# Row maxima as bias and 64-column exponentials for the second block of local attention, in a fused attention and squared-ReLU kernel

## The chip, the cores and the metric

One core of one Trainium2 chip runs the kernel. The metric is the device time of one execution in microseconds. The kernel before was timed in 3 runs: 785.89, 786.21 and 788.44 us, median 786.21 us.

## What is computed

```python
# attention within chunks of 64 tokens: B, H, S, D = 8, 8, 576, 64
scores = scale * np.matmul(q_c, k_c.transpose(0, 1, 2, 4, 3))        # scale = 1 / sqrt(64)
scores = scores - np.max(scores, axis=-1, keepdims=True)
attn = np.exp(scores)
attn = attn / (np.sum(attn, axis=-1, keepdims=True) + 1e-09)
out = np.matmul(attn, v_c)
...
# then on x = out as 4608 tokens x 512
h = x @ w_in                                                          # 512 -> 2048
r = np.maximum(h, 0.0)
g = s * (r * r) + b
return (g @ w_out).astype(np.float32)                                 # 2048 -> 512
```

## The kernel before

All matrix products keep fp32 accuracy: the weights and the tokens are each split into a high part `hi` and a low part `lo`, and a product is three matmuls. The 4608 tokens go through in columns of 512. The first 512 are done in a start-up stage (`Layer`: `up0` to `up15`, `down0` to `down15`) while the weights come in from HBM and are converted: `load` (DMA), `scale` and `tail` (ScalarE), `shift` and `sign` (VectorE), `add` (GpSimd), `hi` (ScalarE), `lo` (VectorE). Sixteen loads k = 0 to 15 are converted in this way, the first in halves `0a` and `0b`. The raw words lie in a pool of 3 buffers, so that `load3` waits until `add0a` and `add0b` have read load 0. The converted weights are written back to HBM (`in`, `out` steps, by DMAs on SyncE's queue) and streamed from there for the 4096 remaining tokens, which are done in four blocks of 1024 with seven products in the place of eight.

The softmax of the first 512 tokens can't hide behind earlier matmuls. It is done by two objects of class `Early`: `one` (tokens 0 to 255) and `two` (tokens 256 to 511), each in two halves i = 0 and 1 of 128 tokens with 8 heads. The steps of a half are: `scores` (TensorE, 32 matmuls of 64x64, line 464), `peak` (VectorE, the row maximum, line 470), `sub` (VectorE, scores less maximum, PSUM to SBUF, line 476), `exp` (ScalarE, one instruction of 128x512, line 480), `sum` (VectorE, line 486), `normz` (VectorE, two small instructions, lines 490 and 491), `norm` (VectorE, line 495), `transposes` (TensorE, line 504), `copies` (ScalarE, line 509), `values` (TensorE, line 516), and `x_hi` (ScalarE, line 524) with `x_lo` (VectorE, line 528), which give the split tokens that the up products read. `up0a` and `up1a` are the up products of columns 0 to 255 (they need `one`), `up0b` and `up1b` of columns 256 to 511 (they need `two`).

PSUM has 8 banks of 512 fp32 columns. At the start they are: `ps_p`, two pairs; `ps_a`, one pair; `ps_h`, two single banks. A half's scores take 256 columns in each bank of a pair, so that the two halves of a block share their two banks; the second half's scores wait until the reader of the first half's has done, since an instruction waits for users of the same bank. `one.scores` and `one.values` use the first pair of `ps_p`, `two.scores` and `two.values` the second, the transposes of both use `ps_a`.

The order of the work is written out by hand: `ORDER` (lines 19 to 73) is a list of names, called one by one, and each engine runs its own instructions in that order. `keep_busyN` (line 124) issues N matmuls of 128x128 on constant data that nobody reads; each of the N shows as two records in the trace. `s_and_b` puts the scalars s and b on all partitions by two tiny transposes on TensorE, and `sb` copies them out on VectorE. Loads and stores are issued by SyncE in the order of the list; a store that waits holds what stands behind it.

Of the kernel before, what the change touches and what calls it, by code (L numbers as in the profile page):

```python
# [30 lines left out]
g_hi3 three.norm down0 scale4 g_lo1 hi3 shift4 relu2 g_lo3 three.transposes sign4 square2
g_hi2 down1 load6 lo3 tail5 scale5 add4 g_lo2 in2 three.copies up4 shift5
hi4 sign5 tail6 load7 four.scores lo4 relu4 scale6 add5 up5 out1 four.peak
square4 five.load_qk g_hi4 four.sub hi5 shift6 down2 load8 g_lo4 relu5 sign6 tail7
scale7 lo5 three.values four.exp add6 in3 square5 up6 four.sum three.x_out g_hi5 shift7
hi6 g_lo5 down3 sign7 relu6 square6 four.normz g_hi6 load9 add7 tail8 g_lo6
up7 scale8 four.norm hi7 lo7 four.transposes relu7 square7 load10 shift8 up8 scale9
in4 lo6 four.copies sign8 g_hi7 tail9 down4 shift9 out2 add8 g_lo7 relu8
square8 tail10 up9 g_hi8 sign9 load11 hi8 g_lo8 add9 scale10 down5 relu9
square9 g_hi9 shift10 hi9 lo8 five.scores sign10 out3 down6 scale11 load12 five.peak  # L40
six.load_qk add10 tail11 g_lo9 five.sub down7 hi10 shift11 lo9 five.exp sign11 in5
four.values lo10 tail12 up11 add11 five.sum scale12 load13 five.load_v out4 four.x_out five.normz
hi11 up10 shift12 five.norm x21.hi relu11 sign12 x11.hi down8 x21.lo relu10 square11
add12 square10 load14 g_hi11 g_hi10 five.transposes g_lo11 scale13 g_lo10 down9 five.copies x11.lo
hi12 shift13 lo11 tail13 six.scores sign13 in6 up13 lo12 scale14 add13 six.peak
load15 out5 tail14 seven.load_qk six.sub up12 relu13 square13 shift14 ring0 six.exp s_add1
hi13 down10 sign14 relu12 g_hi13 lo13 square12 tail15 add14 g_lo13 five.values in7
g_hi12 six.sum scale15 down11 g_lo12 five.x_out six.normz shift15 hi14 six.load_v six.norm up14
sign15 ring1 lo14 up15 add15 out6 relu14 square14 g_hi14 g_lo14 hi15 down12
s_add0 ring2 s_hi1 lo15 s_hi0 s_add7 relu15 six.transposes out7 square15 down13 g_hi15  # L50
s_add5 six.copies s_lo0 six.values s_lo1 s_keep0 g_lo15 down14 six.x_out s_add6 s_keep1 x22.hi
xt1.add_dve seven.scores x22.lo xt1.hi seven.load_v down15 xt3.add_dve eight.load_qk xt1.lo xt3.hi xt2.add_dve p1.0
st2 st1 xt3.lo xt2.hi p2.0 seven.peak u1.0 st0 p1.1 xt2.lo st3 c11.0
p5.0 u1.1 xt4.add_dve relux.0 p6.1 s_add3 xt4.hi p6.0 u2.1 seven.sub p7.1 xt4.lo
ring3 u2.0 seven.exp s_add2 p7.0 u3.1 p2.1 seven.sum u3.0 c22.0 p4.0 seven.normz
c11.1 p3.0 s_add4 c21.0 relux.1 sqx.0 p4.1 ring4 c12.0 seven.norm s_hi2 p1.2
c21.1 s_lo2 split0.hi p5.1 seven.turn0 s_keep2 u1.2 sqx.1 p6.2 reluy.0 c22.1 p2.2
split0.lo u2.2 ring5 sqy.0 seven.turn1 p3.1 split1.hi p7.2 c11.2 s_hi3 seven.turn2 relux.2
p1.3 ring6 u3.2 c12.1 p4.2 seven.turn3 reluy.1 p5.2 u1.3 sqy.1 s_lo3 seven.values
eight.scores ring7 c21.2 c22.2 sqx.2 s_keep3 split1.lo p3.2 seven.x_out eight.peak eight.load_v nine.load_qk  # L60
p2.3 eight.sub s_hi4 c12.2 p6.3 eight.exp c11.3 reluy.2 eight.sum p5.3 ring8 relux.3
s_lo4 sqy.2 p1.4 eight.normz u2.3 s_keep4 eight.norm p2.4 u1.4 eight.turn0 p6.4 p7.3
c11.4 u2.4 eight.turn1 relux.4 p7.4 u3.3 c22.3 p4.3 u3.4 eight.turn2 p3.3 ring9
c21.3 sqx.3 eight.turn3 p1.5 s_hi5 c12.3 p4.4 ring10 s_lo5 u1.5 reluy.3 p5.4
s_keep5 c21.4 sqy.3 eight.values nine.scores c22.4 sqx.4 p3.4 eight.x_out nine.load_v nine.peak p6.5
nine.sub s_hi6 ring11 c12.4 p2.5 nine.exp s_lo6 reluy.4 p1.6 c11.5 ten.load_qk s_keep6 u2.5
nine.sum relux.5 p7.5 sqy.4 nine.normz u1.6 p5.5 nine.norm u3.5 nine.turn0 p4.5 ring12
# [1138 lines left out]
```

## Time and profile before

| | |
|---|---|
| median of 3 runs | 786.21 us |
| the profiled execution's own time | 787.31 us |
| its span (first to last instruction) | 785.3 us |
| TensorE busy | 772.5 us, 98% |
| VectorE busy | 615.6 us, 78% |
| ScalarE busy | 470.2 us, 60% |
| GpSimd busy | 48.6 us, 6% |
| matmuls of the up product j = 1, columns 256 to 511, start | 31.52 us |

An engine's busy time is an average over very different stages. The instructions that the change adds and removes run in the first 35 us; so the tables by stretch and the engines' instructions in order of time are read for the start. Times in rows are in us from the start of the span unless marked ns; the duration of an instruction reaches past the start of the next one on the same engine where the two overlap, so that the distance between starts ("pitch") is what an engine pays in a row of instructions.

### The profile page before, as it was taken

Reading aid. Unit: us, or ns where it says so; the run is one execution under the profiler, and the core shown is the slowest. Engines: PE = TensorE matmul, PEld = TensorE weight load, DVE = VectorE, ACT = ScalarE, POOL = GpSimd, SP = SyncE. Lnnn points to the kernel's source line nnn. Section 1 sums busy time; section 2 is a strip of 40 time slices with the busy share of each in tenths; the row PEclk is TensorE's granted clock in tenths of the full one; section 3 lists DMA queues with packets and bytes.
Section 4 is the critical chain, followed back from the end, with each engine's and each line's share of the span. In section 5 each row is a group of like instructions: output and inputs, shape, how many; then the busy total and the mean of one; then the engine's idle time right before and its main releaser. Section 6 shows DMA issues by size and latency. Waiting matters only on the chain.

```text
span 785.3 us, 13873 instructions
## 1 busy us (share of the span) xinstructions
PE 772.5 (98%) x5584; PEld 639.2 (81%) x5584; DVE 615.6 (78%) x891; ACT 470.2 (60%) x645; POOL 48.6 (6%) x23
## 2 busy tenths in 40 slices
PE   6899999999999999999999999999999999999998
PEld 6787887888888888888888888888888888888886
DVE  5998999998569986888899858888998723348773
ACT  3899877777653433566864635666846346565442
POOL 1443440000000000000000000000000000000000
PEclk9999999999999999999999999999999999999999
DMA  9999998778568999876566587666565778886653
GB/s 360 343 349 337 362 314 307 234 241 270 183 218 293 307 352 332 320 269 222 181 214 208 194 299 290 247 260 205 175 224 179 243 262 293 297 269 214 206 195 135
DMA packets 79844, 204.33 MB, mean 260 GB/s; under 512 B 5796, under 2 KB 39076, under 8 KB 68516
## 3 DMA queue, kind: packets, MB, share of 16 engines
q1 hardware_dynamic: 79488, 203.18, 74.4%
q8 instruction: 44, 0.72, 0.4%
q10 hardware_dynamic: 292, 0.26, 0.1%
q14 instruction: 20, 0.16, 0.1%
HBM read 159.38 MB, written 44.04 MB: 259 GB/s over the span
## 4 chain that ended last, share of the span: by engine, by line
PE 83%; DMA 6%; DVE 5%; ACT 3%; issue 1%; POOL 0%; POOLq 0%; SPq 0%; DVEq 0%; ACTq 0%
PE ps_h L690 22%; PE ps_h L910 17%; PE ps_o L690 17%; PE ps_x L910 8%; PE ps_x L609 6%; PE ps_o L910 4%; PE ps_h L609 3%; PE ps_o L609 3%; DMA raw<-in_w_dram 2%; PE ps_a L368 1%; PE ps_x L424 1%; DMA w_in<-t 1%; DVE t L198 1%; DMA w_out<-t 1%; DVE t L182 1%; ACT t L172 1%
## 5 line engine op out<-in xcount | busy, mean ns | idle before, releaser
L690 PE MATMUL ps_h<-t,raw 128*128 128x512 f32 x672 | 167.4, 391 | 0.0
L690 PEld LDWEIGHTS ps_h<-t,raw 128*128 128x128 f32 x672 | 125.4, 188 | 26.5 <-ACT u L700 0.2
L910 PE MATMUL ps_h<-t,raw 128*128 128x512 f32 (+1 forms) x588 | 142.4, 385 | 0.0
L884 DVE TENSOR_TENSOR t<-t 128x512 fp32r<-128x512 f32 (+1 forms) x120 | 105.5, 900 | 33.2 <-ACT t L882 33.1
L910 PEld LDWEIGHTS ps_h<-t,raw 128*128 128x128 f32 x588 | 108.8, 188 | 22.2
L709 DVE TENSOR_TENSOR t<-ps_o,u 128x512 f32<-128x512 f32 x96 | 66.0, 690 | 75.7 <-PE ps_o L690 70.3
L690 PE MATMUL ps_o<-t,raw 128*128 128x512 f32 x480 | 121.8, 389 | 0.0
L690 PEld LDWEIGHTS ps_o<-t,raw 128*128 128x128 f32 x480 | 90.1, 188 | 18.8
L700 ACT COPY u<-ps_h 128x512 f32<-128x512 f32 x96 | 56.0, 585 | 69.5 <-PE ps_h L690 68.6
L882 ACT CAST t<-t 128x512 fp32r<-128x512 f32 (+1 forms) x120 | 87.4, 789 | 2.8 <-PE ps_h L910 1.9
L412 DVE STREAM_TRANSPOSE pT<-p 32x256 f32<-32x256 f32 x192 | 83.7, 436 | 3.2
L910 PE MATMUL ps_x<-t,raw 128*128 128x512 f32 x288 | 73.2, 390 | 0.0
L753 ACT ACTIVATE t<-t 128x1024 f32<-128x1024 f32 x64 | 67.2, 1053 | 0.2
L910 PEld LDWEIGHTS ps_x<-t,raw 128*128 128x128 f32 x288 | 54.0, 188 | 11.5 <-DMA raw<-w_out 0.3
L749 ACT ACTIVATE t<-t 128x512 f32<-128x512 f32 (+1 forms) x64 | 54.1, 846 | 10.3 <-DVE t L709 9.8
L190 POOL TENSOR_TENSOR t<-t,raw 128x1024 int32<-128x1024 int32 (+1 forms) x17 | 47.9, 2820 | 69.0 <-DVE t L184 39.1
L609 PE MATMUL ps_x<-t,raw 128*128 128x512 f32 x192 | 48.9, 390 | 0.0
L634 PE MATMUL ps_h<-x,t 128*128 128x512 f32 (+1 forms) x216 | 47.5, 371 | 1.3 <-DVE x L528 0.7
L914 ACT ACTIVATE u<-ps_h,shift,sb 128x512 f32<-128x512 f32 x18 | 13.1, 779 | 58.2 <-PE ps_h L910 58.2
L634 PEld LDWEIGHTS ps_h<-x,t 128*128 128x128 f32 x216 | 37.0, 188 | 8.9 <-DVE x L528 1.0
L609 PEld LDWEIGHTS ps_x<-t,raw 128*128 128x128 f32 x192 | 36.0, 188 | 7.5
L910 PE MATMUL ps_o<-t,raw 128*128 128x512 f32 x144 | 36.5, 389 | 0.0
(129 smaller groups left out, 1014.7 us busy)
## 6 DMA issues: line engine op xcount, KB each, us to landing
raw<-w_in SPq DMA_DIRECT2D x42, 1024.0 KB, 6.0
raw<-w_out SPq DMA_DIRECT2D x34, 1024.0 KB, 5.3
raw<-w_sum SPq DMA_DIRECT2D x24, 1024.0 KB, 5.0
raw<-in_w_dram SPq DMA_DIRECT2D x15, 1024.0 KB, 7.9
qk<-in_qkv_dram SPq DMA_DIRECT2D x15, 1024.0 KB, 8.2
w_out<-t SPq DMA_DIRECT2D x16, 512.0 KB, 6.6
w_sum<-t SPq DMA_DIRECT2D x16, 512.0 KB, 9.1
v<-in_qkv_dram SPq DMA_DIRECT2D x15, 512.0 KB, 4.6
```

What stands on the lines that cost most here:

```text
L190: nc.gpsimd.tensor_tensor(out=i, in0=i, in1=low.bitcast(I32), op=ALU.add)
L412: nc.vector.transpose(out=self.pT[k].rearrange("p i a t -> p (i a) t")[:, :, t], in_=p[t, :, k])
L609: nc.tensor.matmul(out=self.ps[m], lhsT=x, rhs=y, start=(j == 0 and i == 0), stop=(j == stop and i == 2))
L634: nc.tensor.matmul(out=self.ps[j][:, cols], lhsT=w[:, c, :], rhs=x[:, c, :], start=(c == 0 and i == 0), stop=(c == NHP - 1 and i == 2))
L690: nc.tensor.matmul(out=ps, lhsT=w[:, e, :], rhs=y[:, e, :], start=start and e + i == 0, stop=e + i == 3, skip_group_check=not start)
L700: nc.scalar.copy(out=u, in_=self.a[p])
L709: nc.vector.tensor_tensor(out=self.tile(p, h)[:, e, :], in0=ps, in1=u, op=ALU.add)
L749: nc.scalar.activation(out=t, in_=t, func=AF.Relu)
L753: nc.scalar.activation(out=t, in_=t, func=AF.Square)
L882: nc.scalar.copy(out=hi, in_=f)
L884: nc.vector.tensor_tensor(out=lo, in0=f, in1=hi.bitcast(F32), op=ALU.subtract)
L910: nc.tensor.matmul(out=self.acc[name][m][:, cols], lhsT=x, rhs=y[:, cols], start=new and q == 0, stop=q == 2, skip_group_check=not new)
```

## The change

For `two`, the subtraction, the one wide exponential and the sum are replaced. VectorE forms `less`, the row maxima times -1/8 (`bias`, 128x8). ScalarE then makes eight exponentials of 128x64 for each half (`exps`), which read the scores from PSUM, take a column of `less` as bias and write the row's sum through `accum_out`. In `one`, the second half's scores go to a bank pair of their own (`ps_a`, which `one.transposes` uses afterwards), so that they need not wait for `one.sub0`. `two`'s halves still share a pair. `ORDER` is new throughout its length. Its start, both versions, follows; behind it the steps are the same, in a somewhat other order.

```diff
-one.load_qk0 one.load_qk1 three.load_qk load0b load0a two.load_qk0 two.load_qk1 two.load_v one.scores0 one.peak0 one.load_v s_and_b
-sb one.sub0 one.exp0 one.scores1 keep_busy7 load1 one.sum0 one.peak1 three.load_v one.normz0 one.sub1 one.norm0
-one.exp1 four.load_v tail0b one.transposes0 keep_busy3 one.sum1 one.normz1 one.copies0 load2 one.norm1 tail0a scale0a
-one.transposes1 four.load_qk shift0a scale0b two.scores0 keep_busy8 one.copies1 sign0a shift0b add0a two.peak0 two.sub0
-hi0a sign0b two.scores1 two.exp0 lo0a add0b two.peak1 one.values0 keep_busy7 two.sum0 one.x_hi0 two.sub1
-load3 hi0b one.x_lo0 two.exp1 lo0b one.values1 keep_busy4 tail1 two.normz0 in0 two.sum1 scale1
-two.norm0 two.normz1 two.transposes0 keep_busy2 one.x_hi1 shift1 two.copies0 two.norm1 two.values0 sign1 two.transposes1 two.x_hi0
-one.x_lo1 two.copies1 add1 two.x_lo0 up1a scale2 tail2 two.values1 shift2 up0a hi1 sign2
-two.x_hi1 three.scores lo1 add2 two.x_lo1 in1 three.peak scale3 up1b tail3 three.sub up0b
...
+one.load_qk0 one.load_qk1 two.load_qk0 two.load_qk1 four.load_v four.load_qk load0a load0b one.load_v one.scores0 one.peak0 load1
+one.scores1 keep_busy3 s_and_b sb one.sub0 one.peak1 one.exp0 two.load_v two.scores0 keep_busy13 one.sum0 one.sub1
+load2 one.normz0 one.exp1 two.peak0 one.sum1 two.bias0 one.normz1 two.exps0 one.norm0 three.load_v one.transposes0 keep_busy1
+one.norm1 one.transposes1 three.load_qk one.copies0 two.normz0 two.scores1 keep_busy2 one.copies1 two.norm0 scale0a two.peak1 two.transposes0
+keep_busy7 tail0a shift0a two.bias1 sign0a two.exps1 add0a one.values0 keep_busy7 scale0b two.normz1 hi0a
+shift0b one.x_hi0 two.norm1 tail0b lo0a two.transposes1 keep_busy4 scale1 sign0b one.x_lo0 tail1 add0b
+one.values1 keep_busy6 shift1 hi0b load3 one.x_hi1 lo0b two.copies0 sign1 in0 scale2 two.values0
+one.x_lo1 two.copies1 add1 two.x_hi0 up0a tail2 two.x_lo0 two.values1 shift2 hi1 up1a sign2
+two.x_hi1 three.scores lo1 add2 two.x_lo1 in1 scale3 three.peak up1b tail3 three.sub up0b
...
         def scores(self, i):
-            if i == 0:
-                self.ps = self.banks(0)
+            if i == 0 or self.tb == 0:
+                self.ps[i] = self.banks(i)
+            else:
+                self.ps[i] = self.ps[0]
...
+        def bias(self, i):
...
+            nc.vector.tensor_scalar(out=self.less[:, i], in0=self.m[:, i], scalar1=-1.0 / float(D) ** 0.5, scalar2=None,
+                                    op0=ALU.mult)
+
+        def exps(self, i):
...
+            for g in range(NHP):
+                for c in range(2):
+                    n = 2 * g + c
+                    nc.scalar.activation(out=self.p[:, i, g, c, :], in_=self.ps[i][:, c, i, g, :], func=AF.Exp,
+                                         scale=1.0 / float(D) ** 0.5, bias=self.less[:, i, c, g:g + 1],
+                                         accum_out=self.z[:, i, n:n + 1])
```

## Rows read from the trace of the kernel before

**Rows 1.** The page's first lines: span, and busy us (share of the span) with the count of instructions of each engine.

```profile
span 785.3 us, 13873 instructions
PE 772.5 (98%) x5584; PEld 639.2 (81%) x5584; DVE 615.6 (78%) x891; ACT 470.2 (60%) x645; POOL 48.6 (6%) x23
```

**Rows 2.** Busy time by stretch: stretch, its length, busy us of each engine with the number of instructions, granted TensorE clock (1.00 is the higher of its levels), busy share of the DMA engines, GB/s.

```profile
15.00:20.00 5.00, 4.47 (x93) 4.07 (x91) 4.96 (x10) 2.57 (x5) 3.01 (x2) 1.00 1.02 413
20.00:25.00 5.00, 3.67 (x82) 3.14 (x82) 4.93 (x12) 3.85 (x7) 0.00 (x0) 1.00 1.03 422
35.00:40.00 5.00, 5.00 (x23) 3.96 (x22) 4.93 (x7) 5.00 (x9) 3.31 (x1) 1.00 0.96 365
140.00:160.00 20.00, 20.00 (x90) 16.21 (x88) 19.60 (x36) 14.92 (x21) 0.00 (x0) 1.00 0.62 199
```

**Rows 3.** TensorE's matmuls in order of time: start, duration of the whole piece, line, tile, count, and in brackets the idle time before it with what ended it.

```profile
4.53 1.13 PE L464 MATMUL ps_p<-t 64*64 64x64 f32 x32 [4.53 <-DMA t<-in_qkv_dram]
5.59 0.36 PE L1105 MATMUL ps_h<-ident,sb_row 1*128 1x1 f32 x2
7.20 1.13 PE L464 MATMUL ps_p<-t 64*64 64x64 f32 x32 [1.25 <-DVE t L476]
8.26 3.35 PE L126 MATMUL ps_h<-t 128*128 128x128 f32 x14
11.41 1.06 PE L504 MATMUL ps_a<-ident,t 128*128 128x128 f32 x4
...
14.54 2.05 PE L126 MATMUL ps_h<-t 128*128 128x128 f32 x16
17.13 0.69 PE L464 MATMUL ps_p<-t 64*64 64x64 f32 x32 [0.53 <-DVE t L476]
...
31.52 8.47 PE L634 MATMUL ps_h<-x,t 128*128 128x256 f32 x47 [0.29 <-DVE x L528]
...
67.69 2.55 PE L634 MATMUL ps_h<-x,t 128*128 128x512 f32 x10 [0.53 <-DVE t L198]
...
123.96 1.16 PE L424 MATMUL ps_a<-pT,v 64*64 64x64 f32 x64 [0.42 <-ACT pT L417]
```

**Rows 4.** VectorE's instructions in order of time, columns as in rows 3: from the first maximum to the first norm; the first conversion after a pause; the last two ahead of the up product at 31.52.

```profile
5.73 0.69 DVE L470 TENSOR_REDUCE m<-ps_p 128x8 f32<-128x512 f32 x1 [4.73 <-PE ps_p L464]
6.34 0.15 DVE L1168 COPY sb<-ps_h 128x2 f32<-128x2 f32 x1
6.46 0.69 DVE L476 TENSOR_TENSOR t<-ps_p,m 128x512 f32<-128x512 f32 x1
...
9.04 0.16 DVE L490 TENSOR_SCALAR z<-z 128x8 f32<-128x8 f32 x1
...
9.36 0.64 DVE L476 TENSOR_TENSOR t<-ps_p,m 128x512 f32<-128x512 f32 x1
9.92 0.68 DVE L495 TENSOR_TENSOR t<-t,z 128x512 f32<-128x512 f32 x1
...
14.25 0.43 DVE L182 TENSOR_SCALAR t<-t 128x512 uint32<-128x512 uint32 x1 [1.70 <-ACT t L172]
...
29.64 1.22 DVE L198 TENSOR_TENSOR t<-t 128x1024 fp32r<-128x1024 f32 x1
30.78 0.69 DVE L528 TENSOR_TENSOR x<-ps_p,x 128x512 fp32r<-128x512 f32 x1
```

**Rows 5.** ScalarE's instructions in order of time: `one.exp1` with the conversion behind it, one wide `tail`, and `two.x_hi1`.

```profile
10.03 0.63 ACT L480 ACTIVATE t<-t 128x512 f32<-128x512 f32 x1 [2.22 <-DVE t L476]
10.57 0.66 ACT L176 ACTIVATE raw<-raw 128x512 int32<-128x512 uint32 x1
...
27.08 1.16 ACT L176 ACTIVATE raw<-raw 128x1024 int32<-128x1024 uint32 x1
...
29.07 0.58 ACT L524 CAST x<-ps_p 128x512 fp32r<-128x512 f32 x1
```

**Rows 6.** ScalarE's groups by line and shape over the whole span: count, busy us, mean ns of one, idle before. The first two read PSUM with fixed numbers for scale and bias, the last two take both from columns in SBUF.

```profile
L700 ACT COPY u<-ps_h 128x512 f32<-128x512 f32 x96 | 56.0, 585 | 69.5 <-PE ps_h L690 68.6
...
L440 ACT COPY t<-ps_a 128x256 f32<-128x256 f32 x8 | 2.4, 393 | 1.3 <-PE ps_a L424 1.3
...
L914 ACT ACTIVATE o<-ps_h,shift,sb 128x512 f32<-128x512 f32 x4 | 3.1, 779 | 15.3 <-PE ps_h L910 14.7 <-DMA raw<-w_in 0.6
...
L942 ACT ACTIVATE o<-ps_h,shift,sb 128x256 f32<-128x256 f32 x2 | 1.1, 567 | 8.5 <-PE ps_h L910 8.5
```

**Rows 7.** GpSimd's instructions in order of time: `add0a`, `add1`, `add2`.

```profile
15.55 1.34 POOL L190 TENSOR_TENSOR t<-t,raw 128x512 int32<-128x512 int32 x1 [14.25 <-DVE t L184]
...
25.47 2.43 POOL L190 TENSOR_TENSOR t<-t,raw 128x1024 int32<-128x1024 int32 x1 [6.06 <-DVE t L184]
29.86 3.30 POOL L190 TENSOR_TENSOR t<-t,raw 128x1024 int32<-128x1024 int32 x1 [1.95 <-DMA raw<-in_w_dram]
```

**Rows 8.** SyncE's DMA issues in order of time (start, time to issue, line, tile): the q and k of `one`, and `load3`. The lines of times to landing are those of the two loads of `one` (least, median, greatest) and of `load3`.

```profile
0.74 0.85 SPq L452 DMA_DIRECT2D t<-in_qkv_dram  x2
...
19.44 0.33 SPq L157 DMA_DIRECT2D raw<-in_w_dram  x1
...
DMA to landing us min/median/max: 3.7/4.2/4.6
...
DMA to landing us min/median/max: 10.4/10.4/10.4
```

More of the change, by code (lines that the diff above doesn't have):

```diff
@@ L25 @@
-load3 hi0b one.x_lo0 two.exp1 lo0b one.values1 keep_busy4 tail1 two.normz0 in0 two.sum1 scale1
-two.norm0 two.normz1 two.transposes0 keep_busy2 one.x_hi1 shift1 two.copies0 two.norm1 two.values0 sign1 two.transposes1 two.x_hi0
-one.x_lo1 two.copies1 add1 two.x_lo0 up1a scale2 tail2 two.values1 shift2 up0a hi1 sign2
-two.x_hi1 three.scores lo1 add2 two.x_lo1 in1 three.peak scale3 up1b tail3 three.sub up0b
-open_o load4 relu1 shift3 hi2 up3 sign3 relu0 three.exp lo2 square0 square1
-add3 three.sum out0 up2 g_hi0 relu3 g_hi1 load5 square3 three.normz tail4 g_lo0
@@ L31 @@
[L31 to L67, printed above, removed]
@@ new lines @@
+one.x_lo1 two.copies1 add1 two.x_hi0 up0a tail2 two.x_lo0 two.values1 shift2 hi1 up1a sign2
+two.x_hi1 three.scores lo1 add2 two.x_lo1 in1 scale3 three.peak up1b tail3 three.sub up0b
+open_o load4 relu1 hi2 shift3 up3 sign3 relu0 three.exp lo2 square0 square1
+add3 three.sum out0 g_hi0 up2 relu3 g_hi1 load5 square3 tail4 g_lo0 three.normz
+down0 hi3 g_lo1 three.norm scale4 g_hi3 lo3 relu2 three.transposes square2 shift4 in2
+g_hi2 down1 g_lo3 three.copies sign4 tail5 load6 g_lo2 add4 scale5 up5 shift5
@@ new lines @@
+hi4 sign5 four.scores relu5 square5 lo4 load7 scale6 up4 five.load_qk add5 four.peak
+out1 g_hi5 tail6 g_lo5 four.sub down2 relu4 hi5 shift6 sign6 load8 square4
+scale7 lo5 three.values four.exp add6 in3 g_hi4 up7 four.sum three.x_out g_lo4 tail7
+shift7 hi6 up6 four.normz sign7 relu7 square7 four.norm g_hi7 down3 add7 g_lo7
+relu6 load9 scale8 tail8 lo6 square6 four.transposes hi7 shift8 out2 down4 g_hi6
+lo7 four.copies load10 g_lo6 in4 scale9 sign8 five.scores tail9 shift9 add8 up9
+five.peak five.sub six.load_qk hi8 sign9 up8 five.exp load11 lo8 tail10 add9 five.sum
@@ new lines @@
+out3 scale10 down5 relu8 relu9 square8 five.normz square9 shift10 four.values hi9 five.norm
+g_hi9 down6 sign10 g_hi8 five.load_v four.x_out lo9 load12 scale11 add10 g_lo8 in5
+x11.hi five.transposes g_lo9 x21.hi up10 five.copies shift11 x11.lo tail11 sign11 down7 hi10
+relu10 x21.lo square10 load13 scale12 add11 up11 tail12 g_hi10 shift12 hi11 lo10
+six.scores relu11 square11 sign12 out4 tail13 down8 load14 lo11 seven.load_qk g_hi11 scale13
+add12 g_lo10 in6 six.peak up12 g_lo11 six.sub hi12 shift13 down9 six.exp lo12
@@ new lines @@
+relu12 square12 sign13 scale14 up13 six.sum load15 add13 g_hi12 out5 tail14 g_lo12
+down10 shift14 hi13 ring0 s_add1 relu13 square13 lo13 g_hi13 five.values sign14 in7
+tail15 down11 six.normz add14 g_lo13 scale15 five.x_out six.load_v up15 shift15 hi14 six.norm
+ring1 sign15 up14 s_hi1 lo14 relu15 add15 square15 out6 g_hi15 down12 relu14
+g_lo15 square14 g_hi14 s_add6 ring2 hi15 six.transposes g_lo14 lo15 down13 six.copies s_add4
+out7 s_lo1 six.values s_add5 s_keep1 down14 six.x_out s_add0 x22.hi seven.load_v xt1.add_dve seven.scores
@@ new lines @@
+s_hi0 x22.lo xt1.hi down15 eight.load_qk xt3.add_dve s_lo0 xt3.hi xt2.add_dve s_keep0 p1.0 st2
+st1 xt3.lo st3 p2.0 xt2.hi xt1.lo st0 p1.1 u1.0 xt2.lo p5.0 u1.1
+c11.0 s_add2 relux.0 p6.0 xt4.add_dve p2.1 ring3 u2.0 s_add3 xt4.hi p7.0 xt4.lo
+p6.1 u3.0 c11.1 c22.0 p4.0 relux.1 s_add7 u2.1 p3.0 c21.0 seven.peak sqx.0
+p1.2 ring4 c12.0 s_hi2 seven.sub p7.1 reluy.0 s_lo2 u1.2 p5.1 sqy.0 s_keep2
+seven.exp p6.2 split0.hi seven.sum p2.2 u2.2 ring5 split0.lo u3.1 p7.2 c11.2 c22.1
+relux.2 p4.1 seven.normz u3.2 seven.norm p3.1 c21.1 seven.turn0 sqx.1 p4.2 ring6 s_hi3
@@ new lines @@
+c12.1 p1.3 split1.hi s_lo3 c21.2 p5.2 split1.lo reluy.1 s_keep3 sqx.2 seven.turn1 p1.4
+sqy.1 p2.3 ring7 c22.2 u1.3 seven.turn2 p6.3 c11.3 p3.2 u2.3 seven.turn3 relux.3
+p7.3 s_hi4 ring8 c12.2 seven.values eight.scores s_lo4 u3.3 u1.4 reluy.2 s_keep4 sqy.2
+p5.3 eight.peak seven.x_out p6.4 eight.load_v eight.sub nine.load_qk c22.3 p4.3 eight.exp u2.4 eight.sum
+p3.3 ring9 c21.3 sqx.3 eight.normz p7.4 eight.norm s_hi5 c12.3 p1.5 u3.4 eight.turn0
+reluy.3 p2.4 u1.5 sqy.3 s_lo5 p4.4 ring10 c11.4 s_keep5 eight.turn1 p6.5 relux.4
@@ new lines @@
+c21.4 sqx.4 p5.4 eight.turn2 u2.5 p1.6 c22.4 p2.5 eight.turn3 p3.4 c11.5 relux.5
+p7.5 ring11 c12.4 s_hi6 u1.6 p5.5 s_lo6 u3.5 reluy.4 eight.values nine.scores s_keep6
+c22.5 sqy.4 p6.6 ring12 eight.x_out nine.peak nine.load_v p2.6 nine.sub ten.load_qk u2.6 p3.5
+nine.exp c11.6 relux.6 nine.sum p7.6 s_hi7 c12.5 p4.5 nine.normz u3.6 s_lo7 reluy.5
+p4.6 ring13 c21.5 nine.norm sqy.5 s_keep7 p1.7 nine.turn0 sqx.5 p5.6 c21.6 u1.7
+nine.turn1 sqx.6 p6.7 ring14 c22.6 p2.7 u2.7 nine.turn2 p7.7 c11.7 p3.6 nine.turn3
@@ L73 @@
+relux.7 u3.7 d0 ring15 c12.6 reluy.6 p5.7 sqy.6 p4.7 c22.7 p3.7 c21.7
+sqx.7 c12.7 ring16 reluy.7 sqy.7
 """
@@ L463, in scores @@
                     qk = self.qk[i]
-                    nc.tensor.matmul(out=self.ps[cols, c, i, hp, :], lhsT=qk[rows, 0, h, :], rhs=qk[rows, 1, h, :],
+                    nc.tensor.matmul(out=self.ps[i][cols, c, i, hp, :], lhsT=qk[rows, 0, h, :], rhs=qk[rows, 1, h, :],
                                      start=True, stop=True)
@@ L469, in peak @@
                 self.m = att.tile([P, 2, G], F32, name="m%d" % self.tb).rearrange("p i (c g) -> p i c g", c=2)
-            nc.vector.tensor_reduce(out=self.m[:, i], in_=self.ps[:, :, i], op=ALU.max, axis=AX.X)
+            nc.vector.tensor_reduce(out=self.m[:, i], in_=self.ps[i][:, :, i], op=ALU.max, axis=AX.X)
         def sub(self, i):
@@ L475, in sub @@
                 self.p = t.rearrange("p i (g c k) -> p i g c k", g=NHP, c=2)
-            nc.vector.tensor_tensor(out=self.p[:, i].rearrange("p g c k -> p c g k"), in0=self.ps[:, :, i],
+            nc.vector.tensor_tensor(out=self.p[:, i].rearrange("p g c k -> p c g k"), in0=self.ps[i][:, :, i],
                                     in1=self.m[:, i].unsqueeze(3).to_broadcast([P, 2, NHP, CH]), op=ALU.subtract)
@@ L498, in norm_pool @@
             self.norm(i, nc.gpsimd)
+        def bias(self, i):
+            if i == 0:
+                t = self.t = slot()
+                self.p = t.rearrange("p i (g c k) -> p i g c k", g=NHP, c=2)
+                self.less = att.tile([P, 2 * G], F32, name="less%d" % self.tb).rearrange("p (i c g) -> p i c g", i=N, c=2)
+            nc.vector.tensor_scalar(out=self.less[:, i], in0=self.m[:, i], scalar1=-1.0 / float(D) ** 0.5, scalar2=None,
+                                    op0=ALU.mult)
+        def exps(self, i):
+            if i == 0:
+                self.z = att.tile([P, 2 * G], F32, name="z%d" % self.tb).rearrange("p (i g) -> p i g", i=N)
+            self.p3 = self.t.rearrange("p i (g k) -> p i g k", k=CH)
+            for g in range(NHP):
[4 more added lines that the diff above has]
+                                         accum_out=self.z[:, i, n:n + 1])
         def transposes(self, i):
@@ L1135, in local_attention_then_squared_relu_mlp @@
         if isinstance(a, Early):
-            for f in steps + ["load_qk", "x_hi", "x_lo"]:
+            for f in steps + ["load_qk", "x_hi", "x_lo", "bias", "exps"]:
                 for i in range(2):
```

7 lines of the change are left out of this document (1 added, 6 removed).

## The prediction

> **What bounds the kernel now.** First the page's busy shares: TensorE 98% of 785.3 us [rows 1]. Then the table by stretch, to see where it isn't: 20.00 of 20 us from 140 to 160, but 4.47 and 3.67 of 5 in 15 to 25 [rows 2]. Part of that is `keep_busy`, which computes nothing. Third, TensorE's order of time: behind the up product at 31.52 the idle pieces that I read are 0.53 us at 67.69 and 0.42 at 123.96 [rows 3]. So the time is that of the start, up to the up product of `two`'s columns (`up1b`, 31.52), plus a fixed stream. What moves 31.52 moves the end one for one, unless the two later waits give some of it back.
>
> What sets 31.52? It waited 0.29 us for `two.x_lo1` on VectorE, which ran behind `lo1` (29.64 and 30.78) [rows 3, 4]. VectorE was busy 4.96 and 4.93 of 5 us in 15 to 25 while ScalarE had 2.57 and 3.85 [rows 2]. VectorE is the bound of the start, ScalarE has slack. The change moves softmax work from the one to the other.
>
> **Removed from VectorE.** Two `sub` and two `sum` at a pitch of 0.60 (0.69 for one less 0.09 of overlap [rows 4]) are 2.4 us; two `bias` of 128x8 come in at 0.15 (the 128x8 row has 0.16 [rows 4]). Net 2.1 us less in a stretch without holes: the whole of the possible gain.
>
> **Added to ScalarE.** Two `exp` go (0.54 of pitch, 10.03 to 10.57 [rows 5]); sixteen exponentials of 128x64 come. No such row exists. From PSUM with fixed numbers, 512 columns take 585 ns and 256 take 393 [rows 6]: 0.75 per column and 201 fixed, so 249 at 64. With scale and bias from columns, 779 and 567 [rows 6]: 408 at 64. One column costs half the difference, so 329; less 0.09 of overlap, a pitch of 0.24. The sum through `accum_out` is in no row. Free would be 0.24; an instruction of its own, at most another shortest one (0.25), makes 0.49. A result of one column should lie nearer to the fixed part less overlap (0.11) than to 0.25: I take 0.14, so 0.38, 3.05 us for eight. Bounds 1.9 and 3.9. A gain below 0.24 is excluded, as the fixed part is paid by every row.
> The Trainium skill, ScalarE: Activation LUTs, What ACT_TABLE_LOAD costs, gives 280 ns plus 0.833 per column with a bias column and 93 ns of overlap, so an estimate of 1.9 us for eight, and no price for the sum. By it the sum below would end 2 us earlier; it is the low end reached from rows anyway, and still over three times one wide `exp`.
>
> **The bank pair, and what stands in its way.** Before, `one.scores1` waited 1.25 us for `one.sub0` [rows 3]. Now it follows `one.scores0` at once: 0.74 plus half of 0.85 for its issue, 4.6 to land [rows 8], so 5.8, and done at 6.9 (pitch 1.06, 4.53 to 5.59 [rows 3]). But the new list puts `keep_busy3` before `s_and_b`, and `sb` before `one.sub0` on VectorE. Six records at 0.225 (14 in 8.26 to 11.41 [rows 3]) end at 8.2, `s_and_b` (0.36 [rows 3]) at 8.6. VectorE, through with `peak0` at 6.4, stands until then, and `sub0` and ScalarE's `exp0` behind it: `sub0` at 8.7, not 6.46 [rows 4]. This is 2.2 us later, with the wait of 1.25 gone.
>
> **Walk to the new up product.** VectorE from 8.7: `peak1` 9.3, `sum0` 10.1 (after `exp0`: 0.69 + 0.63 [rows 4, 5]), `sub1` 10.7, `normz0` 11.3 (0.32, 9.04 to 9.36 [rows 4]), `two.peak0` 11.6, `sum1` 12.2, `bias0` done 13.0; `normz1`, `norm0`, `norm1` to 14.6. In the kernel before, VectorE stood 1.70 us ahead of 14.25 [rows 4], so the late start is absorbed up to here and two steps of `two` are done as well. From 13.0 the work is ScalarE's, in its order, with 0.5 for a narrow copy (0.58 less 0.09), 0.57 for a narrow and 1.05 for a wide conversion (0.66 and 1.16 less overlap) [rows 5]: `exps0` to 16.05, two copies 17.05, `scale0a` and `tail0a` 18.2 (`bias1` is ready then), `exps1` 21.2, `scale0b` and `hi0a` 22.3, `x_hi0` and `tail0b` 23.3, `scale1` and `tail1` 25.4. `hi0b` needs `add0b`: `lo0a`, `sign0b` on VectorE to 24.1, GpSimd 1.4 (1.34 [rows 7]), so 25.6 to 26.2. `x_hi1` and `two.copies0` 27.2, `scale2` 28.2, `copies1` and `two.x_hi0` 29.2, `tail2` 30.3. `hi1` needs `add1`: `lo0b` at 26.3, `sign1` to 28.1, GpSimd 2.43 or 3.30 [rows 7], mean 2.87, so 31.0; `hi1` 32.0, `lo1` on VectorE 32.1 to 33.25, `two.x_lo1` 33.95. Up product at 34.0 for 31.52: **+2.45 us**. With 0.24 in the place of 0.38 the same walk ends at 32.0 (+0.45; 31.5 and 0.0 with the short add), with 0.49 at 35.8 (+4.3; +4.7 with the long add). Even without any wait ScalarE's own work from 13.0 to `two.x_hi1` is 18.7 us at 0.38 and 16.5 at 0.24.
>
> **What costs nothing, and its cover.** Loads: `load0a` is now the eighth 512 KB, `two.load_v` the thirteenth, `load2` ends with the fifteenth, `three.load_qk` with the eighteenth. At 413 GB/s [rows 2] each takes 1.27 us after the first at 4.5: 13.4, 19.7, 22.3, 26.1. They are wanted at 17.0 (`scale0a`), 28 (`values0`), 27.2 (`scale2`) and after 31. `load3` waits for `add0b`, 25.6 in the place of 19.44, with `in0`, `in1` and `load4` behind it on SyncE's queue. It took 10.4 us then [rows 8], in a queue of 20 units that lasts to 28.6; from 25.6 it lands about 31, before `scale3` (33). If it took 10.4 again, the next conversion would lose 3 us. `keep_busy` grows from 31 to 43 calls, all in holes (TensorE waits 1 us before `two.scores1` for `exps0`, with the transposes of `two` queued behind, and 1.4 before `two.transposes1`); the last six end 2 us before `two.x_lo0` is there. `one.transposes0` waits for `sub1`'s release of `ps_a`, at 11.4, and runs at 14.0: free.
>
> **What follows.** Conversion and TensorE start late together, TensorE is full [rows 2], conversion has some slack, so of the two waits (0.95) I count 0.7 as given back: +2.45 - 0.7 = +1.75. The profiled execution took 787.31 with a span of 785.3, 1.1 above the median; its 789.1 is **788.0** against the median of 786.21. 0.3% (2.36 us) is about what a measurement can tell: 783.85 and 788.57 are the edges.
>
> **Rivals.**
> Cheap sums (0.24): +0.45, less all of the 0.95, gives -0.5: 785.7. For it: ScalarE's idle in 15 to 25 [rows 2]; against it: a sum must leave the engine somehow. Chance 0.20.
> Faster: ScalarE never waits for GpSimd or VectorE, and the sums are free. Its own 16.5 us from 13.0 and `x_lo1` (0.7) bring the up product to 30.3, -1.2, and with 0.95 from the later waits -2.2: 784.0, half of it beyond the edge. It decides from a pitch under 0.28. Chance 0.13.
> Slower, sums dear (0.49): +4.3 - 0.7 = +3.6: 789.8. It crosses the edge from a pitch of 0.42. Chance 0.17.
> Slower by the clock: the clock column reads 1.00 in every stretch [rows 2], yet the 128x128 records went at 0.225 before 11.4 and at 0.12 from 14.54 (16 in 2.05 less the last one's tail) [rows 3], as the lower level (1.2 GHz) against 2.4. If the waits before `two.scores1` and `two.transposes1` bring it down again, `keep_busy4`, `values1`, `keep_busy6` and `two.values0` end at 30.4, 1.7 after ScalarE wants `two.x_hi0`; about +1.3 remain at `hi1`: 789.3. Idle 0.53 at 17.13 left the next 32 matmuls at 0.69 us [rows 3], which speaks against. The Trainium skill, TensorE: Matmul & The Clock Gate, What's actually happening, has the clock fall after idleness; no row here shows a fall. Chance 0.05.
> Mine: 0.45.
>
> **How the numbers follow.** Faster: 0.09 of the faster rival and 0.03 of cheap sums, 0.12. Slower: 0.17 and 0.05, and 0.14 of mine (the upper part, pitch over 0.42 or nothing given back), 0.36. The rest, 0.52, is within 0.3%. The range 784.4 to 790.6 leaves out the far half of the faster rival and the far end of the dear sums.
>
> **What would show it.** `sub0` starting near 8.7 behind `sb`; a pitch of `exps` of 0.38 (0.24, 0.49), or a second instruction behind each; ScalarE without holes from 13 to 31; `up1b`'s columns near 34.0; the waits near 67 and 124 smaller. I am wrong if `sb` isn't late, if the up product starts before 32, or if new waits of TensorE stand behind 35 us, where I followed the new list only in outline.

## The result, and the profile after

The changed kernel takes 793.35 us (median of 7 runs, 790.58 to 797.35), the kernel before 786.99 in the same comparison: a ratio of 1.0085, 95% interval 1.0067 to 1.0104, so 6.4 us slower. The forecast of 788.0 had the sign as its second case and missed the size; the time lies above the range. The profiled execution took 791.22 us with a span of 789.2, 3.9 longer than that of before. It is one of the faster executions of the changed kernel, while the profiled one of before (787.31) lies above its median; so the traces show 3.9 us of the 6.4, and where the rest of it goes isn't shown.

TensorE's order of time in the kernel after, with the rows that answer to [rows 3]:

```profile
5.95 1.14 PE L466 MATMUL ps_a<-t 64*64 64x64 f32 x32
7.02 1.65 PE L126 MATMUL ps_h<-t 128*128 128x128 f32 x6
8.59 0.37 PE L1128 MATMUL ps_h<-ident,sb_row 1*128 1x1 f32 x2
...
9.96 4.50 PE L126 MATMUL ps_h<-t 128*128 128x128 f32 x26
...
33.56 8.49 PE L657 MATMUL ps_h<-x,t 128*128 128x256 f32 x47 [0.30 <-DVE x L551]
...
98.68 2.97 PE L657 MATMUL ps_h<-x,t 128*128 128x512 f32 x12 [0.40 <-DVE t L678]
...
133.64 1.52 PE L713 MATMUL ps_h<-t,raw 128*128 128x512 f32 x6
136.41 1.67 PE L713 MATMUL ps_o<-t,raw 128*128 128x512 f32 x6 [1.26 <-ACT o L636]
...
213.05 1.61 PE L632 MATMUL ps_x<-t,raw 128*128 128x512 f32 x6 [0.30 <-DMA raw<-w_out]
```

The up product of the second 256 columns starts at 33.56 for 31.52 [rows 3], +2.04. The two late waits of before (67.69 and 123.96) are gone, one of 0.40 at 98.68 has come, and the next stage (the first product of the streamed weights, line 713; line 690 before) starts at 133.64 for 131.99, +1.65. Then there are waits that the kernel before hadn't: 1.26 us near 136, and 0.30 for streamed weights near 213. From 220 to 700, TensorE is busy without a hole in both kernels.

VectorE in the start, against [rows 4]; the last two rows shown are `sign2` and `lo1`:

```profile
5.88 0.69 DVE L472 TENSOR_REDUCE m<-ps_p 128x8 f32<-128x512 f32 x1 [4.88 <-PE ps_p L466]
9.00 0.16 DVE L1191 COPY sb<-ps_h 128x2 f32<-128x2 f32 x1 [2.43 <-PE ps_h L1128]
9.08 0.68 DVE L478 TENSOR_TENSOR t<-ps_p,m 128x512 f32<-128x512 f32 x1
...
15.89 0.17 DVE L492 TENSOR_SCALAR z<-z 128x8 f32<-128x8 f32 x1 [1.09 <-ACT t L519]
...
20.65 0.17 DVE L492 TENSOR_SCALAR z<-z 128x8 f32<-128x8 f32 x1 [1.96 <-ACT t L519]
...
30.55 1.23 DVE L184 SCALAR_TENSOR_TENSOR t<-raw,t 128x1024 uint32<-128x1024 uint32 x1
31.69 1.22 DVE L198 TENSOR_TENSOR t<-t 128x1024 fp32r<-128x1024 f32 x1
```

`sub0` starts at 9.08, not 6.46: VectorE stood 2.43 us in front of `sb`. Later it stands 1.09 and 1.96 us for ScalarE's exponentials, where it had been back to back. From 28.59 on it is back to back again.

ScalarE, first two and last of the first eight exponentials, the copies that follow, and `hi1`:

```profile
13.38 0.31 ACT L519 ACTIVATE t<-ps_p,less 128x64 f32<-128x64 f32 x1 [0.98 <-DVE less L508]
13.59 0.19 ACT L519 ACTIVATION_READ_ACCUMULATOR t<-ps_p,less 128x1 f32 x1
13.68 0.30 ACT L519 ACTIVATE t<-ps_p,less 128x64 f32<-128x64 f32 x1
...
15.42 0.35 ACT L519 ACTIVATE t<-ps_p,less 128x64 f32<-128x64 f32 x1
15.62 0.24 ACT L519 ACTIVATION_READ_ACCUMULATOR t<-ps_p,less 128x1 f32 x1
15.71 1.11 ACT L532 COPY pT<-ps_a 128x512 f32<-128x512 f32 x2
...
30.00 1.06 ACT L194 CAST t<-t 128x1024 fp32r<-128x1024 f32 x1 [0.39 <-POOL t L190]
```

Eight take 2.33 us (13.38 to 15.71), a pitch of 0.29. The row's sum is an instruction of its own, 0.19 to 0.24 us long, but it starts 0.1 us before the exponential's record ends.

### The profile page after: what moved, and what is told of

It reads as the page before. It is cut to its first block, busy times and chain, and to the rows that moved or that the text cites. A ratio compares the mean times of both kernels' runs of the same rounds, so it can differ in the third digit from the quotient of the medians.

```text
span 789.2 us, 13945 instructions
## 1 busy us (share of the span) xinstructions
PE 776.5 (98%) x5608; PEld 641.9 (81%) x5608; DVE 612.0 (78%) x889; ACT 474.1 (60%) x675; POOL 47.7 (6%) x23
## 4 chain that ended last, share of the span: by engine, by line
PE 85%; DVE 6%; ACT 4%; DMA 4%; issue 1%; SPq 0%; DVEq 0%; ACTq 0%
PE ps_h L713 22%; PE ps_h L933 17%; PE ps_o L713 16%; PE ps_x L933 8%; PE ps_x L632 6%; PE ps_o L933 4%; PE ps_o L632 3%; PE ps_h L632 3%; PE ps_h L657 2%; DMA w_out<-t 2%; PE ps_a L368 1%; PE ps_x L424 1%; DVE t L198 1%; DMA raw<-in_w_dram 1%; DVE t L184 1%
```

## The experiments

Theory A: the start costs everything, and later waits only follow from it. Theory B: the start costs about 2 us, the new order behind it the rest. Within B, B1 says that each new wait costs its own length, B2 that sums, splits and streamed weights are late by the amount of work and only show in turn; theory C came later and names one misplaced step. "Rest" is the list from `open_o` on. "Up product" is the start of `up1b`, as in the prediction.

| kernel | median us | ratio to before, 95% | up product | next stage | span of the profile |
|---|---|---|---|---|---|
| before (profile shown) | 786.2 | | 31.52 | 131.99 | 785.3 |
| after | 793.35 | 1.0085 (1.0067 to 1.0104) | 33.56 | 133.64 | 789.2 |
| `new_again` | 792.43 | 1.0072 (1.0060 to 1.0083) | 33.84 | 133.20 | 790.4 |
| `new_start_old_rest` | 789.03 | 1.0030 (1.0021 to 1.0040) | 33.35 | 132.98 | 786.6 |
| `old_start_new_rest` | 793.45 | 1.0088 (1.0075 to 1.0101) | 31.42 | 132.88 | 789.6 |
| `softmax_alone` | 792.29 | 1.0074 (1.0055 to 1.0093) | 36.16 | 136.30 | 790.1 |
| `banks_alone` | 786.04 | 0.9995 (0.9984 to 1.0005) | 30.58 | 131.37 | 784.6 |
| `sb_first_old_rest` | 787.59 | 1.0018 (1.0005 to 1.0031) | 32.39 | 132.65 | 785.9 |
| `st_first` | 793.86 | 1.0085 (1.0067 to 1.0103) | 33.75 | 132.99 | 789.1 |
| `d0_later` | 791.83 | 1.0067 (1.0052 to 1.0081) | 33.53 | 134.22 | 789.3 |
| `s_hi1_later` | 790.26 | 1.0050 (1.0034 to 1.0065) | 33.15 | 132.53 | 786.9 |
| `s_hi1_early_in_old` | 789.91 | 1.0042 (1.0028 to 1.0056) | 31.32 | 133.09 | 786.6 |
| `repaired` | 787.17 | 1.0010 (0.9994 to 1.0025) | 31.30 | 129.95 | 783.8 |
| `exps_128` | 786.75 (one execution) | | 30.64 | 131.51 | 784.6 |
| `old_start_repaired_rest` | 787.51 | 1.0001 (0.9989 to 1.0013) | 30.81 | 129.93 | 783.5 |
| `fewer_busy` | 787.40 | 1.0006 (0.9993 to 1.0020) | 31.38 | 130.55 | 784.6 |

The median of before was 786.35 to 786.99 in the comparisons, so ratios compare better than medians. The markers are of one execution each. The first scores start between 4.37 and 4.78 us in these traces, when q and k have landed, and `new_again` reaches the up product 0.28 us after the same kernel did before; so differences of some 0.4 us in the markers aren't told apart.

**The changed kernel again** (`new_again`), nothing edited.

> The changed kernel once more, nothing edited. Its seven times lay between 790.6 and 797.4 us and the profiled one at 791.2, 3.9 above the profile of before: 2.04 of it at the up product of the second 256 columns, the rest in waits behind 90 us. If the wide spread belongs to the kernel, it comes back (791 to 797, with a granted clock under 1.0 in the long ones); if it was of that chip, the times lie within 2 us of 791.

790.7 to 793.6 us, and 1.59 us of waiting near 214 in the place of 0.30. The slowdown is the kernel's; its size moves by some 3 us from execution to execution. The two longest of the first seven (796.9 and 797.4 us, granted clock 0.997 and 0.998) didn't come back.

**The two halves of the list, crossed** (`new_start_old_rest`, `old_start_new_rest`). The edits in short, the first against the kernel after, the second against the kernel before:

```diff
 # new_start_old_rest: new softmax, bank pair, new list up to up0b
-open_o ... (new rest)
+open_o ... (old rest)
 # old_start_new_rest: old softmax and list up to up0b
-open_o ... (old rest)
+open_o ... (new rest)
```

> The new softmax, bank pair and the new list up to up0b, then the old list from open_o on. Theory A (the start costs it all, and the later waits only follow from a late start): 792 to 794. Theory B (the start costs its 2.0 us, the new order behind 35 us costs the rest): 788.5 to 789.5, with the up product of the second columns near 33.6 and the waits behind 60 us as in the kernel before.

> The old softmax and the old list up to up0b, then the new list. Theory A: as before, 786 to 787.5. Theory B: 789.5 to 792, with the up product at 31.5 and the wait for the store of the first columns near 134 us still there.

The new start alone costs 2.4 us (0.30%), the new rest alone 6.8 (0.88%), with the up product at 31.42, as before. Theory A falls; the new rest costs even more than B's 789.5 to 792. The two don't add up: together they cost what the rest costs alone. In `old_start_new_rest` the next stage starts at 132.88, and TensorE waits behind it as in the kernel after:

```profile
135.65 1.66 PE L690 MATMUL ps_o<-t,raw 128*128 128x512 f32 x6 [1.25 <-ACT o L613]
...
213.44 1.62 PE L609 MATMUL ps_x<-t,raw 128*128 128x512 f32 x6 [1.41 <-DMA raw<-w_out]
```

So with the new rest the next stage starts near 133 with either start. That a late start only takes slack from a rest that is late already fits this, but isn't shown by itself.

**The softmax by itself** (`softmax_alone`).

```diff
-two.sub0 ... two.scores1 two.exp0 ... two.sum0 ... two.sub1 ... two.exp1 ... two.sum1
+two.bias0 ... two.exps0 two.scores1 ... two.bias1 ... two.exps1
```

> The old list, in which only the second block's sub becomes bias, its exp the eight narrow exponentials (the first set ahead of its second scores), and its sum goes; no bank pair. ScalarE pays 2 x (2.33 - 0.54) = 3.6 us more, VectorE 2.1 less. If ScalarE's slack between 15 and 25 us covers it, the up product comes 0.5 to 1.5 us earlier and the time is 785.5 to 786.5; if ScalarE has become the bound of the start whatever the order, the up product comes 1 to 2 us later and the time is 788 to 789.

Worse than either answer: up product at 36.16, +4.6. `two.scores1` shares its banks with the first half's scores, and so waits for all eight exponentials, which stand behind the conversions on ScalarE. TensorE's rows (start, duration, idle), and its clock by stretch (stretch, length, busy us with records, granted clock, DMA share, GB/s):

```profile
14.33 2.05 PE L126 MATMUL ps_h<-t 128*128 128x128 f32 x16
19.94 1.13 PE L466 MATMUL ps_p<-t 64*64 64x64 f32 x32 [3.56 <-ACT t L519]
...
21.85 3.35 PE L126 MATMUL ps_h<-t 128*128 128x128 f32 x14
```

```profile
16.00:20.00 4.00, 0.44 (x8) 0.94 1.00 403
20.00:24.00 4.00, 4.00 (x74) 0.50 1.04 430
24.00:28.00 4.00, 4.00 (x53) 0.71 0.99 399
```

After 3.56 us without work the granted clock is 0.50, its lower level, and the same 32 matmuls take 1.13 us in the place of 0.69 [rows 3]. Here the clock rival is seen; the trace agrees with the Trainium skill, TensorE: Matmul & The Clock Gate, What's actually happening, that idleness brings the clock down. In the changed kernel itself the clock column stays at 1.00 behind its short waits, and 14 constant matmuls still take 1.73 us at 17.64 and 1.83 at 19.92, some 0.12 each.

**The bank pair by itself** (`banks_alone`).

```diff
-            if i == 0:
-                self.ps = self.banks(0)
+            if i == 0 or self.tb == 0:
+                self.ps[i] = self.banks(i)
+            else:
+                self.ps[i] = self.ps[0]
```

> The old list and the old softmax, only that the second half of the first block's scores has the bank pair ps_a, so that it needn't wait for the first sub. The wait of 1.25 us at 7.2 goes. If this wait set the start, the up product of the second columns comes up to 1.2 us earlier (30.3) and the time is 785.4; if the first norm and the conversions set it, as the rows of VectorE say (it is back to back from 14 on), it stays at 31.5 and 786.6.

The up product comes 0.94 us earlier, so the wait of 1.25 set the start for the most part. TensorE then waits 0.81 near 66 and 0.35 near 98 for ScalarE, the next stage comes 0.62 earlier, and the time isn't told from no change.

**`sb` early** (`sb_first_old_rest`).

```diff
-one.scores1 keep_busy3 s_and_b sb one.sub0
+s_and_b sb one.scores1 keep_busy3 one.sub0
```

> The new start with s_and_b and sb put ahead of the first block's second scores and keep_busy3, as they stood in the old list; from open_o on the old list. Against the new start with the old rest (789.0, up product at 33.35): if the 2.4 us for which VectorE stood behind sb are what the start lost, sub0 starts at 6.6, the eight exponentials at 11, and the up product comes at 31.4 to 32, 787 us. If ScalarE's chain and the loads behind it set the start, it comes at 33 and the time stays within 0.5 us of 789.

Between the two answers: the exponentials start at 11.39 and the up product at 32.39, 0.96 us earlier than with `sb` late. The 2.4 us of VectorE didn't all count: ScalarE waited 0.81 us for the first transposes, which stood behind `keep_busy13` until 13.39. The intervals of the two times overlap a little, so the gain in time itself isn't shown clear of noise. In `repaired` and `fewer_busy`, with the same edit and transposes at 12.3 and 12.0, the up product starts at 31.3 and 31.4.

**The waits of the rest, one by one** (`st_first`, `d0_later`).

```diff
 # st_first
-xt3.add_dve s_lo0 xt3.hi xt2.add_dve s_keep0 p1.0 st2 st1 xt3.lo st3 p2.0 xt2.hi xt1.lo st0
+st2 st1 st3 st0 xt3.add_dve s_lo0 xt3.hi xt2.add_dve s_keep0 p1.0 xt3.lo p2.0 xt2.hi xt1.lo
 # d0_later
-d0 ring15 c12.6 reluy.6 p5.7
+p5.7 d0 ring15 c12.6 reluy.6
```

> The new kernel, in which ScalarE copies out the first columns' output right behind the last down product, ahead of two splits of tokens that wait for VectorE; SyncE issues its stores ahead of eight weight stores. The wait of 1.26 us of the second product of the next stage (near 136) goes. Theory B1 (each of the new waits costs its own length): 791.2 for 792.4. Theory B2 (the wait only stands in for VectorE's and the loads' lateness, which the next wait then shows): 792.4, with the wait near 213 longer by as much.

> The new kernel, in which the first down product of the second stage (d0) stands one product later, as in the old list, so that its weights have 1.36 us more to land. Theory B1: the wait for raw<-w_out near 213 (0.3 and 1.6 us in two profiles) goes or falls to 0.2, and the time falls by about 1.0 to 791.4. Theory B2: the streamed weights are late for good, a later product waits in its place, 792.4.

With the copies first, the wait near 136 goes and one of the same size stands two products later, for VectorE:

```profile
137.07 0.39 PE L713 MATMUL ps_o<-t,x 128*128 128x512 f32 x1
138.75 1.43 PE L713 MATMUL ps_o<-t,x 128*128 128x512 f32 x5 [1.29 <-DVE t L593]
```

793.86: nothing gained. B1 falls for this wait; VectorE was late and ScalarE's copies only showed it. With `d0` later the wait near 213 is gone and no other stands in its place, as B1 said, and 791.83 is 0.6 below `new_again`, but the intervals overlap: it may be worth that, it isn't shown.

**What made VectorE late** (`s_hi1_later`, `s_hi1_early_in_old`). Following VectorE back from 136 in the kernel after, the first hole is a long one, and ScalarE's rows show its cause:

```profile
117.03 1.22 DVE L198 TENSOR_TENSOR t<-t 128x1024 fp32r<-128x1024 f32 x1
121.93 0.69 DVE L678 TENSOR_TENSOR t<-ps_h,t 128x512 fp32r<-128x512 f32 x1 [3.68 <-ACT t L674]
```

```profile
115.07 1.08 ACT L194 CAST t<-t 128x1024 fp32r<-128x1024 f32 x1
119.10 1.06 ACT L238 CAST x<-t 128x1024 fp32r<-128x1024 f32 x1 [2.95 <-PE ps_h L657]
120.06 0.58 ACT L662 ACTIVATE u<-ps_h 128x512 f32<-128x512 f32 x1
```

Line 238 is `s_hi1`, a split for the next stage. It writes a tile of the pool that the first tokens lie in, so it waits for the last up product to have read them. The new list has it ahead of `relu15`, whose input `up15` was there some 2.7 us earlier (an estimate: half of the 5.60 us in which TensorE does `up15` and `up14`, from 113.69 on); `relu15`, `square15` and `g_hi15` queue behind it, and VectorE stands 3.68 us at `g_lo15`, with sixteen sums for the next stage queued behind (line 233, to 131). In the old list, where `up15` is the last up product, it stands behind `relu14` and `g_lo14`. Theory C moves this one name in each list:

```diff
 # s_hi1_later (in the new kernel)
-up14 s_hi1 lo14 relu15 add15 square15 out6 g_hi15 down12
+up14 lo14 relu15 add15 square15 out6 g_hi15 s_hi1 down12
 # s_hi1_early_in_old (in the kernel before)
-lo14 up15 add15 out6 relu14 ... ring2 s_hi1 lo15
+lo14 up15 s_hi1 add15 out6 relu14 ... ring2 lo15
```

> The new kernel with one name moved: s_hi1, a split on ScalarE whose tile is free only after the last up product has read the first tokens, goes behind g_hi15 (it stood ahead of relu15, waited 3.23 us for TensorE and held relu15, g_hi15 and, 3.96 us long, VectorE at g_lo15). Theory C (this one wait makes VectorE's sums and splits late, and with them the wait of 1.26 us near 136 and part of the one near 213): VectorE's idle falls under 1 us, the wait near 136 under 0.4, the time is 789.5 to 791 for 792.4. Theory B2 (sums, splits and streamed weights are late by the amount of work): 792 or more, with a wait of the same size a product later.

> The kernel before with the fault alone: s_hi1 right behind the last up product (up15) in the list, ahead of relu14, as the new list has it. Theory C: ScalarE waits some 3 us in it, VectorE behind it, a wait of about 1 us or more appears near 135, 787.5 to 790 for 786.4. Theory B2: no more than 0.5 us, as VectorE's slack covers it: 786.4 to 787.

Both ways as C said. In the new kernel VectorE's hole shrinks to 0.51, the wait near 136 is gone, and 0.47 near 210 remains:

```profile
117.48 0.69 DVE L678 TENSOR_TENSOR t<-ps_h,t 128x512 fp32r<-128x512 f32 x1 [0.51 <-ACT t L674]
```

790.26, some 2 us less than `new_again` (the intervals of the ratios touch, 1.0060 to 1.0065). Put into the kernel before, right behind its last up product and ahead of `relu14`, `s_hi1` costs 3.1 us, clear of noise: ScalarE stands 4.53 us in it, VectorE 5.25, TensorE 2.38.

```profile
116.20 1.05 ACT L238 CAST x<-t 128x1024 fp32r<-128x1024 f32 x1 [4.53 <-PE ps_h L634]
```

```profile
125.10 1.16 PE L424 MATMUL ps_a<-pT,v 64*64 64x64 f32 x64 [2.38 <-ACT pT L417]
```

**The three moves together** (`repaired`: `s_and_b sb` first, `s_hi1` behind `g_hi15`, `d0` later).

> The new kernel with three moves in the list: s_and_b and sb early, s_hi1 behind g_hi15, d0 one product later. If the three causes add up (1.4 of sb, about 2 of s_hi1, 0.6 of d0): 788.5 for 792.4. If what is left of the new order behind 35 us has causes of its own: 790 or more.

787.17, ratio 1.0010 (0.9994 to 1.0025), less than the sum of the three (788.5): all of the loss is gone within what can be told, though three moves out of the whole list are all that was edited. In the trace, which is of the fastest of its twelve executions, the next stage starts at 129.95, 2.0 us earlier than before, but a wait of 0.40 us for streamed weights shows at 182, and the median doesn't show the 2 us.

```profile
129.95 1.52 PE L713 MATMUL ps_h<-t,raw 128*128 128x512 f32 x6
...
182.06 1.63 PE L713 MATMUL ps_h<-t,raw 128*128 128x512 f32 x6 [0.40 <-DMA raw<-w_in]
```

**Fewer, wider exponentials** (`exps_128`, one execution).

```diff
-                for c in range(2):
-                    n = 2 * g + c
-                    nc.scalar.activation(out=self.p[:, i, g, c, :], in_=self.ps[i][:, c, i, g, :], func=AF.Exp,
+                nc.scalar.activation(out=self.p[:, i, g], in_=self.ps[i][:, :, i, g, :], func=AF.Exp,
...
```

> The new start with sb early and the old rest, and each half's eight exponentials of 64 columns merged to four of 128 (both 64-column groups of a pair take the bias of the first, and the even sums hold both; the odd sums are set to 1 by GpSimd, so the softmax of these tokens is not the reference's). ScalarE then pays some 1.4 us for a half in the place of 2.33. If ScalarE's exponentials set what is left of the start's loss, the up product comes 1.0 to 1.9 us earlier than 32.4, at 30.5 to 31.4; if the loads or VectorE set it, at 32 or later.

Four of 128 columns took 1.4 us (10.80 to 12.2). The up product came at 30.64, 1.75 before `sb_first_old_rest`. But its first transposes also ran 1.3 us earlier (12.06); against `repaired`, where they ran at 12.28, it is 0.66 earlier, of which 0.24 is the earlier start of the first scores (4.54 for 4.78). So ScalarE's exponentials may hold part of the start, 0.4 us of it by the fairer pair, for 1.9 us of ScalarE's time; from single executions this isn't shown.

**Two questions left open by then** (`old_start_repaired_rest`, `fewer_busy`).

```diff
 # old_start_repaired_rest: banks_alone up to up0b, then the rest of repaired
 # fewer_busy: repaired with
-two.scores0 keep_busy13
+two.scores0 keep_busy7
```

> The old softmax and the old list up to up0b with the bank pair of its own for the second scores (up product at 30.6 in the run of the bank pair alone), then the new list with s_hi1 and d0 later. If those two moves take away all that was bad in the new order behind 35 us, the next stage starts near 129.5 (98.7 us after the up product, as in the repaired kernel, for 100.5 before) and the time is 783.5 to 785, below both kernels. If the new order keeps costs of its own, 787 or more.

> The repaired kernel with keep_busy7 in the place of keep_busy13 ahead of the first transposes. If the slow constant matmuls cause the spread, they end by 11.5 in all executions, before the first norm is there (12.3), the up product comes at 31.2 and the times lie within 2 us of 786. If the spread has another cause (the loads, the clock in later stages), it stays at 5 us; if the clock falls for want of work, the up product comes at 32 or later.

The repaired rest is no longer worse than the old. Against `old_start_new_rest` only `s_hi1`, `d0` and the bank pair differ, and the ratio falls from 1.0088 to 1.0001; the bank pair alone gave 0.9995. So the two moves together take away what the new rest cost. In the profiled execution the next stage starts at 129.93, 2.06 us before the old kernel's, and the span is 783.5. But the median of 12 is 787.51. That execution was the fastest of its twelve, the trace of before is of an execution above its median, and the forecast of 783.5 to 785 fails; whether the 2 us are there in the other executions isn't shown. With `keep_busy7` the constant matmuls end at 12.0, but the times still spread from 785.7 to 790.6. So the thirteen calls aren't the cause of the spread, and before itself ran from 785.2 to 789.3 in that comparison. The clock stayed at 0.999 to 1.00. No version beat the kernel before beyond its interval.

## Why the prediction was wrong

**`sb` behind `keep_busy3`: right.** Forecast `sub0` at 8.7, measured 9.08, the hole 2.43 us. Its price at the up product is 1 us in `sb_first_old_rest`, where ScalarE next waited 0.81 us for the transposes of `one` behind `keep_busy13`, and some 2 us in `repaired`, where they ran at 12.28.

**The exponentials: mis-sized, inside the bounds.** Taken 0.38, measured 0.29; eight take 2.33 us, not 3.05. From the figures of the Trainium skill, ScalarE: Activation LUTs, What ACT_TABLE_LOAD costs, the prediction had an estimate of 1.9 for eight, without the sums; the trace has 0.30 to 0.35 for one exponential where these figures give an estimate of 0.33, and the read of the sum on top.

**The walk: near in its result, in part by luck, as errors offset each other.** Forecast 34.0, measured 33.56. The lower pitch made it earlier, by 1.4 us over the sixteen exponentials; `sub0` 0.4 later and VectorE's order at the end made it later. ScalarE was the bound from 13 to 28.6, as forecast: VectorE's holes of 1.09 and 1.96 us are for it. From there VectorE is: `hi1` is done at 31.06, and `lo1` starts at 31.69 behind `sign2`, where the walk had it right behind `hi1`. `keep_busy13` ended at 14.4, where 14.0 was forecast, and held nothing in this execution: ScalarE's exponentials run until 15.71, and its copies start at once. ScalarE itself waits 0.4 for `add1`, and 0.49 for `load3` (forecast to be free), the latter behind the steps that the up product needs.

**The give-back: right, for the old order.** Forecast 0.7; in `new_start_old_rest` +1.83 at the up product became +0.99 at the next stage.

**"Plus a fixed stream": the step that failed.** The prediction took the time for that of the start plus a fixed stream. Behind the up product I took the new list for the old one in a somewhat other order and counted nothing for it, and no row was read for the new list's rest. Alone it costs 6.8 us (`old_start_new_rest`). I named this as what would make me wrong, yet gave it no price and no chance. Some 2 to 3 us of it hang on one name: `s_hi1` right behind the last up product cost 3.1 us in the old list, and moved back it gave some 2 in the new one. What was needed was there before the result: line 238 writes the pool of the tokens, the new list puts it directly behind the last up product, and in the trace of before it runs only at 119.20, when the last up product (to 117.21) is done:

```profile
111.61 5.60 PE L634 MATMUL ps_h<-x,t 128*128 128x512 f32 x24
```

```profile
119.20 1.99 ACT L238 CAST x<-t 128x1024 fp32r<-128x1024 f32 x2
```

What is left of the rest's cost is settled only in sum: with `d0` later too it vanishes (`old_start_repaired_rest`), but `d0` by itself isn't told from nothing, so how the cost divides, and whether the two moves act on each other, stays open.

**The rivals.** Cheap sums came nearest in pitch (0.29 against its 0.24) and was as wrong in time; dear sums had the time nearest, 789.8, by a cause that isn't there. The clock rival didn't occur in the changed kernel, but did in `softmax_alone`. That VectorE's relief would surface didn't happen: `repaired` and `fewer_busy` reach the up product at 31.3 and 31.4, `banks_alone` with the old softmax at 30.58. No rival priced the order behind the up product, and all of them lie below 793.35.

## What to carry to other kernels

When a change comes with a new order, the order is a part of the change: cross the halves of the old and the new list first, before explaining any operation. On an engine that runs its instructions in the order of the list, look for one that waits for a buffer, not for data: moved ahead of ready work it delays all that queues behind it, and here the wait showed on another engine, 15 us later, where removing it gained nothing. Replacing one wide instruction by eight narrow ones moved the bound to the engine that got them (0.54 to 2.33 us), and whoever shares a bank with their input waits for the last of the eight (3.56 us in `softmax_alone`).
